# Nine output stores moved from SyncE's queue to GpSimd's in a fused convolution and spectral-mix kernel

## The chip, the cores and the metric

The kernel runs on one core of a Trainium2 chip. The metric is the device time of one launch in microseconds; lower is better. Before the change the median of 7 runs is 176.81 us (176.29 to 177.27).

## What is computed

The inputs are `x` (8 sequences of 3264 positions, 192 channels, float32), `weight` (8 heads, 7 taps) and three matrices of a spectral layer: `w_r` and `w_i` (64 modes, each 192 x 192) and `w_ch` (192 x 192). A causal convolution along the sequence comes first, with the softmax of each head's taps. On its result `x` the spectral layer does this:

```python
X = np.fft.rfft(x, axis=1)
Xr, Xi = (np.real(X[:, :n_modes]), np.imag(X[:, :n_modes]))
Yr = np.einsum('bmd,mde->bme', Xr, w_r) - np.einsum('bmd,mde->bme', Xi, w_i)
Yi = np.einsum('bmd,mde->bme', Xr, w_i) + np.einsum('bmd,mde->bme', Xi, w_r)
Y[:, :n_modes] = Yr + 1j * Yi
y = np.fft.irfft(Y, n=S, axis=1)
u = x + y
return (u + np.maximum(u @ w_ch, 0.0)).astype(np.float32)
```

The output is 8 x 3264 x 192 in float32, 20.05 MB. It is written by the stores that this document is about.

## The kernel before

The 8 sequences are handled as 4 pairs (q = 0 to 3, two sequences each). A sequence has 25 full tiles of 128 positions and one half tile of 64.

The kernel has three stages. First `x` is loaded (line 177), the convolution runs on TensorE (line 351), and the forward transform is collected (line 377) while the convolved tiles stay in SBUF as `xall`. Then the modes' matrices are loaded (line 474) and applied (line 491). Both kinds of load are issued by GpSimd, and the last of them is issued at 96.8 us of the profiled execution. The output stage begins at about 110 us.

The output stage is a loop over 54 items, written out by hand in program order (lines 763 to 786). An item is a bank pair `z` of PSUM. TensorE puts `u @ w_ch` there in two parts (`c_part`, line 576, and the first `m_part`, line 596), ScalarE applies the relu in place (line 661), TensorE adds `y` (the second `m_part`), and `finish(n)` (line 663) lets VectorE add the convolved `x` and write the float32 result to an SBUF buffer, which is then stored. There are four `z`, so TensorE works some items ahead. The items, with the index `n` that the texts use:

- n = 0 and 1: one tile of a pair of sequences, stored by SyncE (line 684), 192 KB each.
- n = 2, 3, 4: the first double tiles. Two neighbouring tiles of one pair; each is stored by two transfers of 192 KB, one for each sequence, issued by SyncE (line 699).
- n = 5 to 51, except 23 and 38: the same tile of two pairs of sequences, stored by one transfer of 384 KB that GpSimd issues (line 694). There are 45 of these. Item 23 has no output (it finishes a table of the inverse transform).
- n = 38, called "h": the half tiles of all 8 sequences. It is stored by four transfers of 96 KB, each from 64 partitions, issued by SyncE (line 675).
- n = 52 and 53: single tiles. Item 52 is stored by GpSimd, item 53 by SyncE (both line 684).

What sets the order around the change: each engine takes its instructions in program order. A store waits on its own engine's queue until VectorE has written the item's buffer (line 686, for "h" line 667). Stores of GpSimd have a further condition: the built program gives eight semaphores in turn to the transfers that GpSimd issues, so that a transfer also waits until the one eight places earlier in that queue has landed. SyncE's transfers have eight semaphores of their own. Buffers of the results (6 at first, 11 at the end, `free` and `LATER`, lines 647 to 656) are used in turn, so VectorE can write into one only when its previous store has landed.

Of the kernel before, what the change touches and what calls it, by code (L numbers as in the profile page):

```python
# [19 lines left out]
def kernel(  # L20
# [9 lines left out]
    nc = tc.nc  # L30
# [137 lines left out]
    def slot(q, t):  # L168
        return NT * q + t
# [55 lines left out]
    for g in range(4):  # L225
        dst, srcv = band[32 * g:32 * g + 32, :, 32 * g:32 * g + PW], pk3[32 * g:32 * g + 32, :, :]
# [225 lines left out]
    for k, u in enumerate(units):  # L452
# [7 lines left out]
        if k:  # L460
            q, t0, n = units[k - 1]
# [196 lines left out]
    def relu(n):  # L658
        duo, zt = items[n]
        w = D * len(duo) if duo[0] != "h" else 2 * D  # L660
        nc.scalar.activation(out=zt[:, :, 0:w], in_=zt[:, :, 0:w], func=ACT.Relu)  # L661

    def finish(n):
        duo, zt = items[n]
        o = buffers[n]
        if duo[0] == "h":
            nc.vector.tensor_tensor(out=o[:, :, :].rearrange("p k (a d) -> p k a d", a=2),
                                    in0=zt[:, :, 0:2 * D].rearrange("p k (a d) -> p k a d", a=2),
                                    in1=xall[:, NF:NF + NT * (NQ - 1) + 1:NT, 0, :].rearrange(
                                        "p (k a) d -> p k a d", k=2), op=ALU.add)  # L670
            for k in range(2):
                for h, r in enumerate(ROWS):
                    dst = bass.AP(tensor=out.tensor, offset=out.offset + ((4 * k + (h ^ k)) * S + P * NF) * D,
                                  ap=[[D, HALF], [2 * S * D, 2], [1, D]])
                    nc.sync.dma_start(out=dst, in_=o[r, k, :].rearrange("p (a d) -> p a d", a=2))
            return
        (q0, t0), (q1, t1) = duo[0], duo[-1]
        s = [slot(*u) for u in duo]
        ov = o[:, :, :].rearrange("p k (i d) -> p (k i) d", i=2)
        if len(duo) == 1:  # L680
            nc.vector.tensor_tensor(out=ov[:, 0:2, :], in0=zt[:, :, 0:D], in1=xall[:, s[0], :, :], op=ALU.add)
            dst = bass.AP(tensor=out.tensor, offset=out.offset + (2 * q0 * S + P * t0) * D,
                          ap=[[D, P], [S * D, 2], [1, D]])
            (nc.sync if n < 2 or n == N - 1 else nc.gpsimd).dma_start(out=dst, in_=ov[:, 0:2, :])
            return
        nc.vector.tensor_tensor(out=o[:, :, :].rearrange("p k (i d) -> p i k d", i=2),  # L686
                                in0=zt[:, :, 0:2 * D].rearrange("p i (k d) -> p i k d", k=2),
                                in1=xall[:, s[0]:s[1] + 1:s[1] - s[0], :, :].rearrange("p k i d -> p i k d"),
                                op=ALU.add)
        if t0 == t1:  # L690

            dst = bass.AP(tensor=out.tensor, offset=out.offset + (2 * q0 * S + P * t0) * D,
                          ap=[[D, P], [S * D, 4], [1, D]])
            nc.gpsimd.dma_start(out=dst, in_=ov)  # L694
        else:
            for i in range(2):
                dst = bass.AP(tensor=out.tensor, offset=out.offset + ((2 * q0 + i) * S + P * t0) * D,
                              ap=[[D, P], [P * D, 2], [1, D]])
                nc.sync.dma_start(out=dst, in_=ov[:, i:4:2, :])

    N = len(duos)
    items = [[duo, None] for duo in duos]
# [60 lines left out]
    for n in range(N + 1):  # L763
        if n < N and not is_zw(n):
            m_part(n, 0)
            relu(n)
        if n + 2 in AHEAD:
            nc.scalar.copy(out=four(items[n + 2][1][:, :, 0:2 * D]), in_=AHEAD[n + 2])
        elif given(n + 2):
            nc.scalar.copy(out=items[n + 2][1][:, :, 0:2 * D].rearrange("p k (a d) -> p k a d", a=2),  # L770
                           in_=halves.rearrange("p (k a) d -> p k a d", k=2))

        if n == 1:
            continue
        if n == 2:
            m_part(0, 1)
            finish(0)

        soon = given(n + 1) or given(n + 2) or given(n + 3) and not given(n - 1)
        if n > 1 and not soon and not given(n):  # L780
            set_up(n + 1)
        if 0 < n and not is_zw(n - 1):
            m_part(n - 1, 1)
            finish(n - 1)
        if n > 1 and soon:
            set_up(n + 2 if given(n + 1) else n + 1)
# [30 lines left out]
```

## Time and profile before

| | us |
|---|---|
| median of 7 runs | 176.81 |
| time of the profiled execution | 176.29 |
| its span, from the first to the last instruction | 174.5 |
| last loads of the modes' matrices issued | 96.8 |
| first and last store issued by SyncE | 111.3, 167.7 |
| first and last store issued by GpSimd | 117.0, 167.8 |
| last work of TensorE and of VectorE | 166.8, 167.7 |

The profile is one execution seen by the hardware profiler. A row of the chain of waits gives the start, the length and the instruction; a row of the table by stretches of time gives each engine's busy time, the granted clock of TensorE, the share of time that the 16 DMA engines were busy, and what they moved. The view of a stretch's DMA queues gives packets, megabytes and the share of the 16 engines' time that the packets took; `software_dynamic` is what GpSimd issues, `hardware_dynamic` what SyncE issues. "Landing" is the time from the start of the issue to the moment when all data is in its place.

### The profile page before, as it was taken

Reading aid. Unit: us, or ns where it says so; the run is one execution under the profiler, and the core shown is the slowest. Engines: PE = TensorE matmul, PEld = TensorE weight load, DVE = VectorE, ACT = ScalarE, POOL = GpSimd, SP = SyncE. Lnnn points to the kernel's source line nnn. Section 1 sums busy time; section 2 is a strip of 40 time slices with the busy share of each in tenths; the row PEclk is TensorE's granted clock in tenths of the full one; section 3 lists DMA queues with packets and bytes.
Section 4 is the critical chain, followed back from the end, with each engine's and each line's share of the span. In section 5 each row is a group of like instructions: output and inputs, shape, how many; then the busy total and the mean of one; then the engine's idle time right before and its main releaser. Section 6 shows DMA issues by size and latency. Waiting matters only on the chain.

```text
span 174.5 us, 6496 instructions
## 1 busy us (share of the span) xinstructions
PE 155.7 (89%) x2818; PEld 112.1 (64%) x2818; DVE 120.6 (69%) x193; ACT 107.2 (61%) x159; POOL 90.4 (52%) x141
## 2 busy tenths in 40 slices
PE   7997989999999997999897696999999999999910
PEld 3554655676666676788674564887786788677700
DVE  1889996847666866466575362788898698788840
ACT  8429878355547335566655242788787787787710
POOL 7999852945634733425334200016758576656650
PEclk9999999999999999999999789999999999999995
DMA  3999999999999999999999991287888989999993
GB/s 45 163 174 192 188 193 191 192 193 193 192 193 193 197 207 207 209 203 207 206 207 206 207 197 25 73 291 308 348 343 331 365 332 358 357 325 353 363 359 131
DMA packets 44077, 40.19 MB, mean 230 GB/s; under 512 B 28544, under 2 KB 40400, under 8 KB 44048
## 3 DMA queue, kind: packets, MB, share of 16 engines
q0 software_dynamic: 40880, 37.58, 108.3%
q1 hardware_dynamic: 3168, 2.19, 3.9%
q8 instruction: 22, 0.36, 0.8%
q14 instruction: 7, 0.06, 0.1%
HBM read 39.40 MB, written 20.05 MB: 341 GB/s over the span
## 4 chain that ended last, share of the span: by engine, by line
DMA 45%; POOL 28%; issue 13%; PE 7%; ACT 1%; DVE 1%; POOLq 1%; ACTq 0%
DMA xall<-in_x_dram 20%; DMA arena<-in_moe_w_i_dram 18%; POOL out_dram L694 16%; POOL xall L177 8%; DMA cc<-in_moe_w_i_dram 7%; PE z L596 4%; PE z L576 3%; PE low L491 1%; ACT z L661 1%; POOL cc L474 1%; POOL xall L258 1%; POOL arena L474 1%; DVE cc L686 1%; POOL early L293 0%; POOLq L812 0%
## 5 line engine op out<-in xcount | busy, mean ns | idle before, releaser
L661 ACT ACTIVATE z<-z 128x768 f32<-128x768 f32 (+1 forms) x53 | 39.8, 770 | 10.3 <-PE z L596 9.4
L596 PE MATMUL z<-mixa,early 64*128 64x384 bf16 (+1 forms) x220 | 33.8, 309 | 0.5 <-ACT z L661 0.4
L596 PE MATMUL z<-mixa,fupper 64*128 64x384 bf16 (+1 forms) x220 | 33.7, 308 | 0.0
L177 POOL DMA_DIRECT2D xall<-in_x_dram x32 | 27.8, 876 | 11.2 <-DMA xall<-in_x_dram 10.2
L369 ACT CAST xall<-z 128x768 bf16<-128x768 f32 (+1 forms) x24 | 20.5, 852 | 19.9 <-PE z L351 19.9
L371 DVE CAST xall<-z 128x768 bf16<-128x768 f32 (+1 forms) x24 | 24.5, 1023 | 10.6 <-PE z L351 10.3
L576 PE MATMUL z<-wc,cc 64*128 64x192 bf16 x504 | 28.4, 243 | 0.0
L351 PE MATMUL z<-xall,band 64*64 64x192 bf16 (+3 forms) x816 | 25.4, 249 | 2.3 <-ACT xall L369 1.4
L576 PEld LDWEIGHTS <-cc 64*128 64x128 bf16 x504 | 22.8, 94 | 5.6 <-issue 2.1
L686 DVE TENSOR_TENSOR arena<-z,xall 128x768 f32<-128x768 f32 x24 | 22.9, 957 | 3.3 <-PE z L596 1.5
L351 PEld LDWEIGHTS <-band 64*64 64x64 bf16 x816 | 16.8, 105 | 10.4 <-issue 5.6
L377 PE MATMUL low<-xall,early 128*128 128x384 bf16 x100 | 20.4, 329 | 0.2 <-ACT early L248 0.2
L686 DVE TENSOR_TENSOR cc<-z,xall 128x768 f32<-128x768 f32 x19 | 18.1, 956 | 3.4 <-PE z L596 2.1
L432 PEld LDWEIGHTS <-xall 128*128 128x128 bf16 x300 | 18.2, 103 | 2.8
L694 POOL DMA_DIRECT2D out_dram<-arena x22 | 16.6, 754 | 6.3 <-DVE arena L686 5.3
L407 DVE COPY cc<-r 128x1024 bf16<-128x1024 bf16 (+2 forms) x22 | 13.3, 633 | 9.5 <-PE r L432 3.7
L694 POOL DMA_DIRECT2D out_dram<-cc x18 | 13.6, 754 | 9.1 <-DVE cc L686 7.2
L596 PEld LDWEIGHTS <-early 64*128 64x128 bf16 x220 | 14.3, 94 | 6.1 <-issue 2.2
L474 POOL DMA_DIRECT2D arena<-in_moe_w_r_dram x12 | 7.4, 613 | 18.3 <-PE low L491 14.6
L694 POOL DMA_DIRECT2D out_dram<-band x5 | 3.8, 759 | 21.0 <-DVE band L686 20.9
L405 ACT COPY cc<-r 128x1024 bf16<-128x1024 bf16 (+1 forms) x11 | 10.1, 915 | 6.2 <-PE r L432 4.0
L596 PEld LDWEIGHTS <-fupper 64*128 64x128 bf16 x220 | 12.1, 94 | 1.3 <-issue 0.2
(129 smaller groups left out, 211.5 us busy)
## 6 DMA issues: line engine op xcount, KB each, us to landing
out_dram<-arena POOLq DMA_DIRECT2D x22, 384.0 KB, 4.8
out_dram<-cc POOLq DMA_DIRECT2D x18, 384.0 KB, 4.8
arena<-in_moe_w_r_dram POOLq DMA_DIRECT2D x12, 288.0 KB, 9.2
arena<-in_moe_w_i_dram POOLq DMA_DIRECT2D x12, 288.0 KB, 10.0
xall<-in_x_dram POOLq DMA_DIRECT2D x6, 480.0 KB, 11.7
xall<-in_x_dram POOLq DMA_DIRECT2D x6, 384.0 KB, 11.2
out_dram<-band POOLq DMA_DIRECT2D x5, 384.0 KB, 4.4
xall<-in_x_dram POOLq DMA_DIRECT2D x8, 192.0 KB, 6.5
```

The source lines that it names most:

```text
L177: nc.gpsimd.dma_start(out=xall[:, s0:s0 + nf, i, :], in_=src)
L351: mm = nc.tensor.matmul(ov[c], band[r, h, c.start + shift + 64 * (r is UP and c is LO): c.start + shift + 64 * (r is UP and c is LO) + 64] ...
L369: nc.scalar.copy(out=dst, in_=srcv)
L371: nc.vector.tensor_copy(out=dst, in_=srcv)
L377: nc.tensor.matmul(xp, ftab[:, t, :], xall[:, slot(q, t), :, :], start=(t == 0), stop=False, skip_group_check=True)
L407: nc.vector.tensor_copy(out=out, in_=in_)
L432: nc.tensor.transpose(tp[:, P * k:P * k + P], src, ident[:])
L576: nc.tensor.matmul(zt[:, i, D * k:D * k + D], cc[r, q, 3 * t + j, :], wc[r, j, :], start=(k == 0 and j == 0), stop=False, skip_group_check ...
L596: nc.tensor.matmul(zt[:, i, D * k:D * (k + w)], tabs[c][r, t, :], zw[r, c, q:q + w, QUARTERS[which], :], start=False, stop=end and k + w = ...
L661: nc.scalar.activation(out=zt[:, :, 0:w], in_=zt[:, :, 0:w], func=ACT.Relu)
L686: nc.vector.tensor_tensor(out=o[:, :, :].rearrange("p k (i d) -> p i k d", i=2), in0=zt[:, :, 0:2 * D].rearrange("p i (k d) -> p i k d", k=2),
L694: nc.gpsimd.dma_start(out=dst, in_=ov)
```

## The change

Nine stores change the engine that issues them. Of the six stores of the items 2, 3 and 4, five go to GpSimd; the first of item 2 stays with SyncE. The four stores of "h" are no longer issued when the item is finished: they are held in a list, and each following call of `finish` (items 39, 40, 41 and 42) lets GpSimd issue one of them just ahead of that item's own store. Nothing else changes: the instructions of TensorE, VectorE and ScalarE are the same in the same order.

```diff
+    held = []
+
     def finish(n):
         duo, zt = items[n]
         o = buffers[n]
@@ -672,8 +675,11 @@
                 for h, r in enumerate(ROWS):
                     dst = bass.AP(tensor=out.tensor, offset=out.offset + ((4 * k + (h ^ k)) * S + P * NF) * D,
                                   ap=[[D, HALF], [2 * S * D, 2], [1, D]])
-                    nc.sync.dma_start(out=dst, in_=o[r, k, :].rearrange("p (a d) -> p a d", a=2))
+                    held.append((dst, o[r, k, :].rearrange("p (a d) -> p a d", a=2)))
             return
+        if held:
+            dst, src = held.pop(0)
+            nc.gpsimd.dma_start(out=dst, in_=src)
         (q0, t0), (q1, t1) = duo[0], duo[-1]
         s = [slot(*u) for u in duo]
         ov = o[:, :, :].rearrange("p k (i d) -> p (k i) d", i=2)
@@ -696,7 +702,7 @@
             for i in range(2):
                 dst = bass.AP(tensor=out.tensor, offset=out.offset + ((2 * q0 + i) * S + P * t0) * D,
                               ap=[[D, P], [P * D, 2], [1, D]])
-                nc.sync.dma_start(out=dst, in_=ov[:, i:4:2, :])
+                (nc.sync if n == 2 and i == 0 else nc.gpsimd).dma_start(out=dst, in_=ov[:, i:4:2, :])
```

## The prediction, made before the changed kernel was run

> **What bounds the kernel now.** I read the page's 40 slices first, then a table of stretches, the chain of waits of the last 25 us, and the DMA queues of single stretches. From 110 us on TensorE is never idle until 166, so it sets the pace of the items; but the span ends only at 174.5. What carries the end is in this table (the columns are busy us with counts, then the granted clock, DMA share and GB/s):
>
> ```profile
> 140.00:152.00 12.00, 12.00 (x200) 8.84 (x196) 10.00 (x12) 9.71 (x13) 7.94 (x12) 1.00 0.93 351
> 154.00:158.00 4.00, 4.00 (x66) 3.01 (x63) 3.24 (x4) 3.44 (x6) 2.24 (x3) 1.00 0.97 325
> 160.00:167.00 7.00, 6.34 (x104) 4.62 (x99) 6.07 (x8) 5.00 (x8) 4.92 (x7) 1.00 0.97 361
> 167.00:172.00 5.00, 0.00 (x0) 0.00 (x0) 0.69 (x2) 0.00 (x0) 1.46 (x2) 0.79 0.91 337
> ```
>
> From 154 us the DMA engines are busy 0.97 of the time, with GpSimd (fifth number) far from full; after 167 nothing works but they, until the last landing near 173.0 (item 52: issued at 167.80, landed 5.1 us later). Then 1.5 us of closing waits. So the end is the drain of a backlog of stores, and TensorE's granted clock is 1.00 as long as it works, so no clock is in play. The second row is odd: as busy as the third, but 325 GB/s in place of 361. It holds the half-tile stores. The chain of waits shows GpSimd's issues there:
>
> ```profile
> 153.98 0.75 POOL out_dram L694
> ...
> 155.01 0.75 POOL out_dram L694
> ...
> 156.16 0.75 POOL out_dram L694
> 156.91 1.24 issue
> 158.14 0.02 POOLq L694
> 158.16 0.53 POOL out_dram L694
> ```
>
> These are items 39 to 42. Asked one by one, their landings took 3.9, 5.5, 5.3 and 4.3 us: they land at 157.9, 160.5, 161.5, 162.5. Items before and after land 1.0 us apart; between 39 and 40 lie 2.55 us. So the half tiles hold up the backlog by 1.55 us, and from there on it never empties: a landing takes 3.5 us where little is queued (item 5, at 117.0), 3.9 for item 39, but 4.3 to 5.5 for all later ones. Why they are so dear is in the queues of three stretches: 112 to 117.5 (SyncE's stores alone), 140 to 150 (GpSimd's alone), 154 to 158 (both):
>
> ```profile
> q1 hardware_dynamic: 2141, 1.55, 84.1%
> ...
> q0 software_dynamic: 970, 3.44, 89.9%
> ...
> q0 software_dynamic: 252, 0.90, 61.4%
> q1 hardware_dynamic: 567, 0.39, 34.5%
> ```
>
> Megabytes over share times length is the rate while engines serve that queue: SyncE's 1.55/(0.841 x 5.5) = 335 GB/s in packets of some 720 B, GpSimd's 3.44/(0.899 x 10) = 383 GB/s in packets of some 3,550 B. Mixed, both are worse: 366 for GpSimd's, 283 for SyncE's.
>
> **Part 1, five early stores (items 2, 3, 4).** SyncE loses five issues, GpSimd gains five of 192 KB; the row for that shape is line 684's issue on GpSimd, 0.71 us. Sum 3.6 us, where GpSimd has been idle since 97.5 us and would first issue at 117.0. VectorE's results are there at 113.0, 114.2 and 115.3, an issue follows 0.28 us later, so the five run at 113.3, 114.5, 115.2, 115.9 and 116.6, and item 5's store starts at 117.3 in place of 117.0. Item 6's (118.1) is on time again. Landings come later: 1.9 to 3.7 us now, 3.5 then (item 5's row). Nobody waits for that: the buffer of item 2 is written again at 119.8 and that of item 3 at 121.1, against landings before 117.6 and 119.5. In the built program's waits these five wait in addition only for weight loads that landed by 107. Cheaper packets save 0.98 MB/335 - 0.98/383 = 0.4 us of DMA time, but at a time when the DMA engines have gaps, and the backlog empties at 130 anyway (the store at 129.99 lands in 2.9 us). I count 0. If item 5's 0.3 us were carried through, the cost is +0.3; below zero there is nothing to gain, since TensorE sets the pace there.
>
> **Part 2, four half-tile stores: issue.** GpSimd gains four issues. The nearest row is line 258's, the same 64 x 2 x 192 shape as a load: 0.604 to 0.647 us; the other bound is 0.71. I take 0.61. Now every instruction past which they are put: item 38's result is there at 152.82. Half 1 runs 153.1 to 153.7; item 39 at 153.98, unmoved; half 2 to 155.34; item 40 at 155.34 (+0.34); half 3 at 156.1; item 41 at 156.7 (+0.56); half 4 at 157.5; item 42 at 158.08, where it starts at 158.16 now, since GpSimd stood idle before it for 1.24 us though VectorE's result was there at 157.2. Items 43 to 46 follow at 158.8, 159.6, 160.45, 161.58: the old times within 0.1. So the 2.4 us of issue fit into GpSimd's gaps, and nothing is late from item 42 on. At 0.71 each, item 42 starts at 158.2 to 158.3, still level.
>
> The waits on the transfer eight places earlier: the tightest is item 46's at 161.6 for item 40's landing, at the latest 160.5. SyncE's last store (item 53, 167.7) has nothing before it in either version. VectorE reuses item 38's buffer near item 49 (163.95); half 4 lands near 161.
>
> **Part 3, the same stores: transfer.** 4 x 96 KB = 0.393 MB at 283 GB/s is 1.39 us of all 16 engines now, at 383 it is 1.03: 0.36 saved. GpSimd's own 0.90 MB of that stretch go at 366 and would go at 383: 2.46 - 2.35 = 0.11. Together 0.47 us out of a backlog that ends the span. The landings say the same from the other side: 1.55 us now against 1.03, so 0.52. I take 0.47.
>
> Here the Trainium skill speaks against the change. "DMA: Bandwidth & Descriptors", section "Issuing engine by pattern", gives a simple store to SyncE's queue as the generally faster one, and its section "Issuing engines are not separate DMA queues" holds that whoever issues, the transfers run on the same 16 engines, so that only issue time is at stake. By it Part 3 is worth 0 and the sum is 0 or a little above. By the rows the engines are the same, but a byte of SyncE's stores occupies them 14% longer (335 against 383 GB/s), 35% longer in the contested stretch. I follow the rows, since the stretch and shape are this kernel's own; untested is that 64-partition stores keep 383 when GpSimd issues them. The bounds for that: 283 (saving only the 0.11) to 383.
>
> **Sum.** 0 (early) + 0 (issue) - 0.47 (transfer) = -0.47 us; span 174.5 to 174.0. The profiled execution took 176.29, 1.8 more than its span, and the median is 0.52 above it; so 175.82 for a like execution, 176.34 for the median.
>
> **Rivals.**
> - No change: the saving is returned. Item 42 is issued no earlier than now (158.08 against 158.16), and the DMA engines can only finish early what has been issued. If 4.3 us is what a landing costs at that load, not 3.9, item 42 lands at 162.4 as now and the tail is the same. Against it: landings of 3.9 and 4.1 (item 37) just before. Without the saving's reach the sum is 0 to -0.1: 176.8.
> - Slower: GpSimd falls behind between items 39 and 42. Twice now it stood still though VectorE's result was there: at 128.65 (issued at 129.99) and at 157.20 (issued at 158.16), about 1.0 and 0.7 us beyond the usual 0.28. I can't name the cause; nine more transfers in the queue may move the place. Today such a pause falls into slack. With four half tiles in the queue there is none: a pause of 1.0 us at item 39 makes item 42 start at 159.1, landing at 159.1 + 3.9 = 163.0 against 162.5. From there the tail keeps its 1.0 us per store, so +0.5 us, 177.3; with 4.3 for the landing +0.9. It decides from a start of item 42 after 158.6 (162.5 - 3.9).
> - The change fails to do what it says: excluded for the order (the built program has the nine transfers in GpSimd's queue as told); that the saving isn't there since the half tiles are slow by their 64 partitions gives -0.1, as the first rival.
>
> **Numbers.** Forecast (saving reaches the end, -0.3 to -0.7): 0.46. No change (within 0.3): 0.29. GpSimd behind (+0.4 to +1.0): 0.25. A measurement of this kernel can tell about 0.2%, or 0.35 us, from no change. Faster by more than that 0.44, within 0.31, slower 0.25. The range takes in the transfer bounds below (176.34 - 0.4) and most of the third case above: 175.9 to 177.5. The likeliest case alone: 176.1 to 176.5.
>
> **What would show it.** Right: in 154 to 158 no packets of SyncE's queue and a rate near 350 GB/s; landings of items 40 to 42 near 4 us; item 42 issued by 158.3; last landing near 172.5. Wrong in Part 3: the same 325 GB/s with GpSimd's packets alone. Wrong in Part 2: gaps or issues of GpSimd that put item 42 past 158.6, and less DMA share in 154 to 160. Wrong in Part 1: VectorE waiting for a landing before 125 us. What would upset all: an item's add waiting for its buffer in the tail, which now never happens.

## The result, and the profile after

The changed kernel has a median of 178.23 us (177.72 to 181.32, 14 runs), against 176.81 for the kernel before (35 runs). The ratio is 1.0095 with an interval of 1.0071 to 1.0118: the change costs about 0.9%, some 1.4 to 1.7 us. The forecast was 176.34 us; the sign was wrong, and the time lies above the range.

Single executions of every kernel here, before's too, scatter by up to some 5 us, and the ratios leave out those more than 1.5% above the fastest of their kernel, which the medians keep. The profiled execution took 181.23 us with a span of 179.5. In it TensorE was granted half its clock from 108.5 to 115.3 us (0.50; in the second profile below 1.00 in the same stretch), just ahead of the output stage, and everything after it is later (VectorE's add of "h" ends at 156.64 in place of 152.82), so that traces are compared below from that add on. These are the stretches that the prediction showed, moved by the same 3.82 us (busy us with counts of PE, PEld, DVE, ACT, POOL, then the granted clock, DMA share and GB/s):

```profile
143.82:155.82 12.00, 12.00 (x200) 8.85 (x196) 10.00 (x12) 9.71 (x13) 7.94 (x12) 1.00 0.91 347
157.82:161.82 4.00, 4.00 (x66) 3.01 (x63) 3.24 (x4) 3.44 (x6) 4.00 (x7) 1.00 0.76 272
163.82:170.82 7.00, 6.34 (x104) 4.61 (x99) 6.07 (x8) 5.00 (x8) 5.32 (x8) 1.00 0.99 363
170.82:175.82 5.00, 0.00 (x0) 0.00 (x0) 0.69 (x2) 0.00 (x0) 1.46 (x2) 0.76 1.00 372
```

The second row tells it (its counterpart, 154:158, is in the prediction). TensorE, VectorE and ScalarE are as busy as before, to the digit. GpSimd went from 2.24 us of work to 4.00 of 4.00. The DMA share fell from 0.97 to 0.76, and the rate from 325 to 272 GB/s. Later the DMA engines are full to the end (0.99 and 1.00). What wasn't moved in the second stretch is moved at the end, after everybody else has stopped. The chain of waits has this for GpSimd:

```profile
155.66 0.75 POOL out_dram L700
156.41 1.18 issue
157.59 0.02 POOLq L700
157.61 0.62 POOL out_dram L682
158.23 0.65 POOL out_dram L700
```

GpSimd stands still for 1.18 us ahead of the first half tile, and from there on issues back to back until item 46's store. Of the 1.24 us at item 42 before, 0.66 were beyond the usual wait for VectorE; this excess has moved here. The queues of 157.82 to 161.82 show a single kind of store:

```profile
q0 software_dynamic: 337, 1.06, 72.4%
```

1.06 MB/(0.724 x 4 us) = 366 GB/s while the engines serve that queue. The two queues together made (0.90 + 0.39)/((0.614 + 0.345) x 4) = 336 before in the same stretch; over the longer stretches used below the gain is gone.

The changed kernel was profiled once more, in an execution without that disturbance (178.30 us, span 176.4). For it and for before, this is the table by which all runs are compared: the 8 us after the add of "h" ends, then the time from VectorE's last add to the end of the span, then two single microseconds, from 1.0 us after the add of "h" on. Before:

```profile
152.82:160.82 8.00, 8.00 (x136) 6.34 (x132) 7.00 (x8) 6.74 (x10) 4.88 (x7) 1.00 0.92 333
167.69:174.50 6.81, 0.00 (x0) 0.00 (x0) 0.00 (x1) 0.00 (x0) 0.82 (x2) 0.66 0.57 212
153.82:154.82 1.00, 1.00 (x18) 0.67 (x16) 0.89 (x1) 1.00 (x3) 0.75 (x1) 1.00 0.92 334
154.82:155.82 1.00, 1.00 (x19) 0.77 (x20) 0.92 (x1) 0.77 (x2) 0.75 (x1) 1.00 0.92 307
```

The changed kernel:

```profile
153.37:161.37 8.00, 8.00 (x136) 6.35 (x132) 7.00 (x8) 6.74 (x10) 7.04 (x11) 1.00 0.81 294
168.24:176.40 8.16, 0.00 (x0) 0.00 (x0) 0.00 (x1) 0.00 (x0) 0.82 (x2) 0.68 0.56 209
154.37:155.37 1.00, 1.00 (x18) 0.67 (x16) 0.89 (x1) 1.00 (x3) 1.00 (x2) 1.00 0.67 269
155.37:156.37 1.00, 1.00 (x19) 0.77 (x20) 0.92 (x1) 0.77 (x2) 1.00 (x3) 1.00 0.59 164
```

From the add of "h" to VectorE's last add it is 14.87 us in both. So nothing is late on the computing engines. GB/s times length says what had still to be moved at the last add: 212 x 6.81 = 1.44 MB before, 209 x 8.16 = 1.71 MB after. The last landing comes 5.26 us after the last add before, and 6.35 after: +1.09 us. Behind the landing lie closing waits, 1.57 us before and 1.85 in both executions of the changed kernel: +0.28. Together 1.37 us, close to the 1.42 between the medians. The first profile of the changed kernel gives 6.11 us for the last landing, with the same 1.71 MB left and 289 GB/s in its 8 us. So the bytes left repeat well, while a difference of 0.2 us in a last landing says nothing.

### The profile page after: what moved, and what is told of

It is laid out like the page before. It is cut to its first block, busy times and chain, and to the rows that moved or that the text cites. A ratio compares the mean times of both kernels' runs of the same rounds, so it can differ in the third digit from the quotient of the medians.

```text
span 179.5 us, 6498 instructions
## 1 busy us (share of the span) xinstructions
PE 157.4 (88%) x2818; PEld 113.2 (63%) x2818; DVE 120.6 (67%) x193; ACT 107.4 (60%) x159; POOL 96.5 (54%) x150
## 4 chain that ended last, share of the span: by engine, by line
DMA 49%; POOL 29%; issue 12%; PE 5%; POOLq 1%; DVE 1%; DVEq 0%
DMA xall<-in_x_dram 25%; POOL out_dram L700 18%; DMA arena<-in_moe_w_i_dram 17%; DMA cc<-in_moe_w_i_dram 7%; POOL xall L177 5%; PE z L596 2%; POOL out_dram L705 1%; PE z L576 1%; POOL out_dram L682 1%; PE low L491 1%; POOL cc L474 1%; POOL arena L474 1%; PE low L606 1%; DVE cc L692 1%; POOLq L818 0%
## 5 line engine op out<-in xcount | busy, mean ns | idle before, releaser
L596 PE MATMUL z<-mixa,early 64*128 64x384 bf16 (+1 forms) x220 | 34.6, 318 | 0.4 <-ACT z L661 0.4
L596 PE MATMUL z<-mixa,fupper 64*128 64x384 bf16 (+1 forms) x220 | 34.4, 317 | 0.0
L576 PE MATMUL z<-wc,cc 64*128 64x192 bf16 x504 | 29.3, 248 | 0.0
L576 PEld LDWEIGHTS <-cc 64*128 64x128 bf16 x504 | 23.5, 96 | 5.8 <-issue 2.4
L700 POOL DMA_DIRECT2D out_dram<-arena x22 | 16.6, 755 | 6.1 <-DVE arena L692 3.7
L705 POOL DMA_DIRECT2D out_dram<-arena x3 | 2.2, 729 | 18.2 <-DVE arena L692 18.2
```

The lines of the kernel that those rows point to most:

```text
L576: nc.tensor.matmul(zt[:, i, D * k:D * k + D], cc[r, q, 3 * t + j, :], wc[r, j, :], start=(k == 0 and j == 0), stop=False, skip_group_check ...
L596: nc.tensor.matmul(zt[:, i, D * k:D * (k + w)], tabs[c][r, t, :], zw[r, c, q:q + w, QUARTERS[which], :], start=False, stop=end and k + w = ...
```

## The experiments

**Theory at the outset.** The loss sits in the half tiles' part: on GpSimd their issues take the place of those of the following items, and the DMA engines get too little to do in the microseconds after the add of "h". **Rivals**: the early stores make it, or their sum with the half tiles does (GpSimd's pause moves); the half tiles are released too late, one by one; the stores of 64 partitions are dear in transfer, whoever issues them.

| kernel | median, us | ratio, interval | last landing after VectorE's last add, us | MB left at that add | GB/s in the 8 us after the add of "h" |
|---|---|---|---|---|---|
| before | 176.81 | | 5.26 | 1.44 | 333 |
| the change again | 178.03 | 1.0076 (1.0041 to 1.0112) | 6.35 | 1.71 | 294 |
| early stores only | 176.76 | 1.0012 (0.9981 to 1.0043) | 5.38 | 1.44 | 322 |
| half tiles only | 177.44 | 1.0022 (0.9995 to 1.0049) | 5.76 | 1.57 | 304 |
| one half tile store of four | 176.97 | 1.0021 (0.9999 to 1.0043) | 4.92 | 1.40 | 297 |
| eight early stores | 178.32 | 1.0085 (1.005 to 1.012) | 6.12 | 1.55 | 312 |
| half tiles in a burst | 177.37 | 1.0045 (1.0022 to 1.0067) | 6.02 | 1.58 | 303 |
| half tiles in eight stores | 178.75 | 1.0138 (1.0094 to 1.0181) | 8.05 | 2.21 | 277 |
| two half tiles on each engine | 177.75 | 1.0022 (0.9993 to 1.005) | 5.29 | 1.44 | 327 |
| half tiles held, on SyncE | 177.03 | 0.9998 (0.9971 to 1.0025) | 5.37 | 1.48 | 326 |
| three early stores | 179.87 | 1.0128 (1.0068 to 1.0188) | 6.95 | 1.80 | 281 |

The third column compares with runs of before on the same chip, whose median was between 176.74 and 176.94. The last three columns come from one execution each. They are counted from the add of "h" or from the last add, so that what happens earlier doesn't touch them; how well they repeat is seen only for the change (6.11 and 6.35 us, 1.71 MB twice, 289 and 294 GB/s).

**The change again.** No edit.

> The changed kernel once more, for a profile whose TensorE clock is not held at half speed for 7 us before the output stage, as in the profile at hand (108 to 115 us). Both theories: 1.0 to 1.6 us above the kernel before. Theory A (the half tiles on GpSimd: the pause of its queue falls at the first half tile, then its issues run back to back until item 45): item 42's store starts about 0.4 us later against VectorE's last add than before, and the last landing comes 0.8 us later against that add. Theory B (the five early stores on GpSimd cost the time): a backlog is seen already between items 5 and 37, landings there longer than before's 4.6 to 4.9 us.

178.03 us; the tables above are from it. Item 42's store starts 9.18 us ahead of the last add, 0.36 later than before, about as expected; the last landing is 0.85 and 1.09 us later in the two profiles, where 0.8 was expected. The row of the half tiles' line 682 shows what its four issues cost (shortest, median and longest in ns):

```profile
L682 POOL DMA_DIRECT2D out_dram<-arena x4: 612/616/621, 154.3 to 158.5; - x4
```

The same view of line 690, whose longest landing is that of item 52 (5.1 before):

```profile
DMA to landing us min/median/max: 2.1/4.2/6.2
```

**Early stores only.**

```diff
-                nc.sync.dma_start(out=dst, in_=ov[:, i:4:2, :])
+                (nc.sync if n == 2 and i == 0 else nc.gpsimd).dma_start(out=dst, in_=ov[:, i:4:2, :])
```

> Only the five stores of items 2, 3 and 4 go to GpSimd; the half tiles stay with SyncE. Theory A: within 0.3 us of the kernel before, since the backlog empties before item 37. It may cost up to 0.8 if the pause of GpSimd's queue, moved to about item 39 by five more transfers, falls where it is not hidden. Theory B: the whole 1.2 to 1.5 us.

176.76 us: no change that can be measured. GpSimd's timeline (start, length, and in brackets the idle time before it and what ended it) at the beginning, and at item 39:

```profile
113.29 0.73 POOL L699 DMA_DIRECT2D out_dram<-arena  x1 [16.18 <-DVE arena L686]
114.46 1.46 POOL L699 DMA_DIRECT2D out_dram<-cc  x2 [0.43 <-DVE cc L686]
115.91 1.45 POOL L699 DMA_DIRECT2D out_dram<-arena  x2
117.36 0.77 POOL L694 DMA_DIRECT2D out_dram<-band  x1
...
154.61 0.75 POOL L694 DMA_DIRECT2D out_dram<-cc  x1 [2.06 <-DVE cc L686]
```

The five issues fill the time up to item 5's store at 117.36, and nothing comes of it at the end. But the pause has moved. Item 39 before the change:

```profile
153.98 0.75 POOL L694 DMA_DIRECT2D out_dram<-cc  x1 [1.39 <-DVE cc L686]
```

GpSimd is now idle for 0.67 us more ahead of item 39, and item 42 waits 0.59 us in place of 1.25. It does no harm here: 1.44 MB are left at the last add, as before. SyncE hands half tiles to the DMA engines in the meantime.

**Half tiles only.** The early stores go back to SyncE; the half tiles stay as in the change.

```diff
-                (nc.sync if n == 2 and i == 0 else nc.gpsimd).dma_start(out=dst, in_=ov[:, i:4:2, :])
+                nc.sync.dma_start(out=dst, in_=ov[:, i:4:2, :])
```

> Only the four half tiles go to GpSimd, one ahead of each of items 39 to 42; the early stores stay with SyncE. Theory A: the greater part of the loss, 0.8 to 1.5 us above the kernel before. Theory B: within 0.3 us of before, or 0.5 faster if the transfer saving of the prediction holds.

177.44 us, less above before than the 0.8 to 1.5 us expected. The ratio's interval takes in 1. The trace has 0.50 us more after the last add, and the lower rate and the bytes left point the same way; the burst below, with the same bytes left, is slower than before beyond its interval.

```profile
152.99:160.99 8.00, 8.00 (x136) 6.32 (x132) 7.00 (x8) 6.74 (x10) 7.32 (x11) 1.00 0.84 304
167.86:175.08 7.22, 0.00 (x0) 0.00 (x0) 0.00 (x0) 0.00 (x0) 0.82 (x2) 0.61 0.59 218
```

So the half tiles cost without the early stores, and the early stores cost nothing that can be measured without the half tiles, but the two together cost more than their sum (0.85 and 1.09 at the last landing against 0.50 + 0.12; 0.27 MB left over before's against 0.13 + 0).

**One half tile store of four.** Before, with three of the four half-tile stores left out, so that this part of the output isn't written.

```diff
-                    nc.sync.dma_start(out=dst, in_=o[r, k, :].rearrange("p (a d) -> p a d", a=2))
+                    if k == 0 and h == 0:
+                        nc.sync.dma_start(out=dst, in_=o[r, k, :].rearrange("p (a d) -> p a d", a=2))
```

> The kernel before with three of the four half-tile stores left out, so that this part of the output is not written; it shows what these stores cost the end when SyncE issues them. If the backlog from the half tiles reaches the end, three quarters of the 1.55 us that the landings showed: 1.0 to 1.2 us faster than before. If the backlog at the end is made later, between items 42 and 53, less than 0.4 us faster.

176.97 us: leaving out 0.29 MB of stores gives nothing that can be measured in the time, and 0.34 us at the last landing of the one profile. The prediction had taken the half tiles for 1.55 us of backlog that is carried to the end. It isn't carried: at the last add 1.40 MB are left, against 1.44.

```profile
168.22:174.70 6.48, 0.00 (x0) 0.00 (x0) 0.00 (x1) 0.00 (x0) 0.82 (x2) 0.67 0.57 216
```

Before the change the DMA engines make good by then what the half tiles add, so that a cheaper transfer of the half tiles could hardly have won 0.47 us.

**Half tiles in a burst.** As half tiles only, with all four issues ahead of item 39's store.

```diff
-        if held:
+        while held:
```

> Half tiles on GpSimd, all four ahead of item 39's store; the early stores on SyncE. Theory A': item 39's store starts 1.5 us later than before and GpSimd's issues bring 160 GB/s for 2.4 us, but from item 42 on the queue is where the interleaved one is: same loss as with one by one, 0.3 to 0.7 us above the kernel before. Rival (the interleaving itself costs): back at the kernel before.

177.37 us, 6.02 after the last add. All four half tiles are released at once, and it is no better than one by one (5.76). These are the four issues here, SyncE's four before, and the microsecond of the burst in which the DMA engines have least to do:

```profile
153.93 2.41 POOL L682 DMA_DIRECT2D out_dram<-arena  x4 [0.53 <-DVE arena L670]
...
152.85 2.67 SPq L675 DMA_DIRECT2D out_dram<-arena  x4
...
156.64:157.64 1.00, 1.00 (x22) 0.85 (x20) 0.62 (x2) 0.96 (x2) 1.00 (x2) 1.00 0.57 136
```

Counted from the add of "h" (153.64 and 152.82) GpSimd's issues end at 2.70 us, and so do SyncE's. The half tiles are no later, and still the kernel is slower: the rival "released too late" falls. With either order GpSimd spends four times 0.6 us on 96 KB each, and the hole in the DMA engines' work only changes its place.

**Half tiles in eight stores.** As half tiles only, each store cut in two of 48 KB, two ahead of each item.

```diff
-                    held.append((dst, o[r, k, :].rearrange("p (a d) -> p a d", a=2)))
+                    src = o[r, k, :].rearrange("p (a d) -> p a d", a=2)
+                    held.append([(dst[:, a:a + 1, :], src[:, a:a + 1, :]) for a in range(2)])
...
-            dst, src = held.pop(0)
-            nc.gpsimd.dma_start(out=dst, in_=src)
+            for dst, src in held.pop(0):
+                nc.gpsimd.dma_start(out=dst, in_=src)
```

> Half tiles on GpSimd cut into eight stores of 48 KB, two ahead of each of items 39 to 42: the bytes are the same, the issue time of GpSimd is doubled (2.4 us more). Theory A': less is moved in the 8 us after the add, by 300 to 500 KB more than with four; 1.5 to 2.2 us above the kernel before. Rival (the cost is in the transfers, not in their issue): within 0.4 us of the half tiles alone.

178.75 us, 8.05 after the last add: the same bytes in twice as many issues cost 2.79 us there in place of 0.50. Eight issues of about 0.53 us take 4.3 us of GpSimd's time in place of 2.5. Over the 8 us only 0.22 MB less are moved than with four (277 against 304 GB/s), where 0.3 to 0.5 were expected; but GpSimd is behind to the end, and at the last add 0.64 MB more are left. A new wait comes on top:

```profile
158.78 0.53 POOL L683 DMA_DIRECT2D out_dram<-arena  x1
159.78 0.54 POOL L683 DMA_DIRECT2D out_dram<-arena  x1 [0.46 <-DMA out_dram<-cc]
160.59 0.77 POOL L701 DMA_DIRECT2D out_dram<-cc  x1 [0.28 <-DVE arena L693]
```

The last half tile waits 0.46 us for a landing: the condition on the transfer eight places earlier, which with small stores in the queue reaches less far back in time.

**Two half tiles on each engine.** The two stores of `k` = 0 stay with SyncE, the two of `k` = 1 go to GpSimd ahead of the items 39 and 40; the early stores stay with SyncE. The list and its use are those of the change (not shown).

```diff
-                    nc.sync.dma_start(out=dst, in_=o[r, k, :].rearrange("p (a d) -> p a d", a=2))
+                    src = o[r, k, :].rearrange("p (a d) -> p a d", a=2)
+                    if k == 0:
+                        nc.sync.dma_start(out=dst, in_=src)
+                    else:
+                        held.append((dst, src))
```

> Two half tiles by SyncE as in the kernel before, two by GpSimd ahead of items 39 and 40; the early stores on SyncE. Theory A': GpSimd has slack for two (1.2 us of issue against gaps of 0.4 us per item); the loss is less than half of that of four: 0 to 0.3 us above the kernel before. Rival (64-partition stores on GpSimd's queue are slow in themselves): half, 0.3 us or more.

5.29 us after the last add, as before, and no difference in the ratio (the median of all 22 executions is 177.75 us, that of the 15 which the ratio takes 176.79). GpSimd's pause is seen at item 41 and costs nothing here:

```profile
157.28 1.50 POOL L704 DMA_DIRECT2D out_dram<-cc  x2 [0.71 <-issue]
```

Two of the four issues fit into GpSimd's gaps, so long as SyncE supplies the DMA engines beside it. It is no gain either.

**Half tiles held, on SyncE.** The order of the change, with SyncE as the issuer; the early stores go back to SyncE too (not shown).

```diff
-            nc.gpsimd.dma_start(out=dst, in_=src)
+            nc.sync.dma_start(out=dst, in_=src)
```

> The order alone: the half tiles' four stores stay with SyncE but are held and issued one by one when the items 39 to 42 are finished; the early stores stay with SyncE. Theory (the loss is GpSimd's issue time: its queue runs back to back and gives the DMA engines too few bytes in the 8 us after the half tiles' add): GpSimd is left alone, so 176.6 to 177.1, last landing 5.2 to 5.6 us after VectorE's last add, about 1.45 MB still to move at that add, and at least 2.5 MB in the 8 us after the half tiles' add. Rival (the loss is that the half tiles are released up to three items later, whoever issues them): 177.3 to 178.0, last landing 5.8 to 6.4, 1.6 MB or more still to move.

177.03 us, as before. It tells less than I had hoped: on SyncE's queue nothing stands between the four stores, so that the order in the program doesn't hold them back:

```profile
153.35 2.75 SPq L682 DMA_DIRECT2D out_dram<-arena  x4
```

They run one after the other from the add of "h" on, as before (152.85, 2.67 us). The run shows only that the order in the program by itself costs nothing; what speaks against the late release is the burst.

**Eight early stores.** The change, with the items 0 and 1 and the first store of item 2 on GpSimd too.

```diff
-            (nc.sync if n < 2 or n == N - 1 else nc.gpsimd).dma_start(out=dst, in_=ov[:, 0:2, :])
+            (nc.sync if n == N - 1 else nc.gpsimd).dma_start(out=dst, in_=ov[:, 0:2, :])
...
-                (nc.sync if n == 2 and i == 0 else nc.gpsimd).dma_start(out=dst, in_=ov[:, i:4:2, :])
+                nc.gpsimd.dma_start(out=dst, in_=ov[:, i:4:2, :])
```

> The changed kernel with three more early stores on GpSimd (items 0 and 1 and the first of item 2), which puts three more transfers ahead of the half tiles. Theory A' (the loss is idle time of the DMA engines in the 8 us after VectorE's add of the half tiles: first because GpSimd issues 96 KB in 0.6 us, second because the pause of GpSimd's queue of about 1.2 us, which comes 24 stores after the former one, falls on the first half tile): the pause moves to about item 36, ahead of the half tiles, so only the first part is left: 0.3 to 0.7 us above the kernel before, as with the half tiles alone. Rival (the early stores add to the loss by themselves, wherever the pause is): 1.2 us or more above, as the changed kernel or worse.

178.32 us: by the ratio 1.5 us above before, which is the rival's outcome (1.2 or more) and not the theory's (0.3 to 0.7). The executions lie in two groups, six from 177.36 to 178.32 and five from 179.43 to 180.53; the profiled one is of the second. The pause did move, to item 36:

```profile
153.48 0.75 POOL L700 DMA_DIRECT2D out_dram<-cc  x1 [1.06 <-DVE cc L692]
```

In half tiles only that item waits 0.39 us:

```profile
150.49 0.75 POOL L700 DMA_DIRECT2D out_dram<-cc  x1 [0.39 <-DVE cc L692]
```

So the pause is 0.67 again, this time ahead of the half tiles. By the bytes this kernel stands where half tiles only stands (1.55 MB left against 1.57), as the theory has it; but the time is that of the change, and the last landing comes 0.36 us later than in half tiles only. So the place of the pause isn't all.

**Three early stores.** The change, with only the second store of item 3 and both of item 4 on GpSimd.

```diff
-                (nc.sync if n == 2 and i == 0 else nc.gpsimd).dma_start(out=dst, in_=ov[:, i:4:2, :])
+                (nc.sync if n == 2 or n == 3 and i == 0 else nc.gpsimd).dma_start(out=dst, in_=ov[:, i:4:2, :])
```

> As the change, but only three of the early stores go to GpSimd (the second of item 3 and both of item 4); the half tiles on GpSimd one by one. The place of GpSimd's 0.68 us pause moves with the data that it has issued before: at the first half tile with five early stores, not seen with none. Theory (the pause among the half tiles makes the difference between 177.4 with none and 178.1 with five): the pause is seen between the second half tile and item 42, last landing 5.9 to 6.4 us after VectorE's last add, 177.8 to 178.4; if it isn't seen, 5.6 to 5.9 and 177.2 to 177.6. Rival (each early store on GpSimd costs by itself, 0.05 to 0.15 us): 177.6 to 177.9 wherever the pause is, and TensorE's last work relative to the first item's add is later than before.

179.87 us, in six runs only, two at 178.4 and four from 179.5 to 180.9; the median is above what theory (178.4 at most) and rival (177.9 at most) gave. 6.95 us after the last add, where five early stores have 6.11 and 6.35. The intervals of the two ratios overlap, so that it isn't shown that three cost more than five; but three don't cost less, and a price per early store is out. The pause is where the theory put it, behind the first half tile; the last line is item 39 in half tiles only:

```profile
155.98 0.62 POOL L682 DMA_DIRECT2D out_dram<-arena  x1 [0.53 <-DVE arena L670]
157.52 0.78 POOL L700 DMA_DIRECT2D out_dram<-cc  x1 [0.91 <-DVE cc L692]
158.29 0.62 POOL L682 DMA_DIRECT2D out_dram<-arena  x1
...
154.15 0.76 POOL L700 DMA_DIRECT2D out_dram<-cc  x1 [0.25 <-DVE cc L692]
```

GpSimd is idle ahead of item 39 for 0.91 us where half tiles only has 0.25: 0.66 more. What it does to the DMA engines:

```profile
155.69:163.69 8.00, 8.00 (x136) 6.34 (x132) 7.00 (x8) 6.74 (x10) 6.79 (x10) 1.00 0.78 281
170.56:179.08 8.52, 0.00 (x0) 0.00 (x0) 0.00 (x1) 0.00 (x0) 0.82 (x2) 0.60 0.57 211
157.70:158.70 1.00, 1.00 (x20) 0.77 (x21) 0.93 (x1) 0.76 (x2) 1.00 (x2) 1.00 0.17 54
```

For one microsecond the DMA engines are busy 0.17 of the time: in the 1.54 us between the issues at 155.98 and 157.52 only 96 KB had been handed to them.

## Why the prediction was wrong, step by step

**What bounds the kernel.** Half right. The span does end with a drain of stores (1.44 MB left at the last add). Wrong was the sentence "the half tiles hold up the backlog by 1.55 us, and from there on it never empties". I read it from landing times of 3.9 to 5.5 us. But a landing is the last of 16 engines: of item 42's data before the change, by the completions that the trace holds, one for each engine, half of the engines had finished 2.8 us after the issue began, and the last at 4.3. The landing told of the slowest engine, not of a store of work on all. The run with one half tile store of four shows what three of the four stores carried to the end: 0.34 us in its profile, and nothing that can be measured in the time.

**Part 1, five early stores: 0.** Right, and close: 113.3, 114.5, 115.2, 115.9, 116.6 and item 5 at 117.3 were predicted; the run with early stores only has 113.29, 114.46, pairs from there to 117.36, and an unchanged time. What was set aside is that these stores move GpSimd's pause.

**Part 2, issue: 0.** This is the step that failed, in its sentence "So the 2.4 us of issue fit into GpSimd's gaps, and nothing is late from item 42 on". Its numbers were nearly right: 0.61 us for an issue (measured 0.616), and in half tiles only the train of issues ran as written to within 0.3 us, item 42 starting 9.46 us ahead of the last add, against 9.53 before. It still cost 0.50 us at the last landing. The mistake was to ask only when GpSimd is level again. Before, SyncE issued the half tiles in 152.85 to 155.52, beside GpSimd's stores of the items 39 and 40; two queues fed the DMA engines. Afterwards GpSimd alone hands over 96 KB in 0.62 us, 160 GB/s, and such issues stand between its large ones. The DMA engines had no backlog to live on (with three early stores their share fell from 0.90 in one microsecond to 0.17 in the next), so that with half tiles only it fell at once, over the 8 us from 0.92 to 0.84. Of the 0.23 MB that were not moved then, 0.13 are still missing at the last add: (1.57 - 1.44) MB at 363 GB/s is 0.36 of the 0.50 us.

**The slower rival** had the right place and mechanism: the pause at item 42 "may move the place", and "with four half tiles in the queue there is none" of the slack that covered it. Its size is near too (+0.5 to +0.9 predicted; from half tiles only to the two profiles of the change +0.35 and +0.59 at the last landing). Its deciding point failed: it asked for item 42 after 158.6, that is less than 9.09 us ahead of the last add, and in the two profiles of the changed kernel that was 9.18 and 9.16 (8.92 only with three early stores). A late start of item 42 isn't needed; too little handed over ahead of it is enough. And the rival took the place of a gain, where in fact it came on top of the half tiles' own loss.

**Part 3, transfer: -0.47.** The second step that failed: the gain isn't there. Rates while the engines are busy, over the 8 us: before (2.26 + 0.39) MB/((0.739 + 0.178) x 8 us) = 361 GB/s, with these rows:

```profile
q0 software_dynamic: 643, 2.26, 73.9%
q1 hardware_dynamic: 576, 0.39, 17.8%
```

Half tiles only has 2.40/(0.835 x 8) = 359, the change 2.33/(0.792 x 8) = 368; the prediction counted on 383. So the half tiles are hardly cheaper with GpSimd's packets than with SyncE's 576. The 283 GB/s that I took for SyncE's came from a stretch of 4 us in which both queues' packets share the engines, and their times include each other's; it was no price of the stores. Even a true saving would have won little, as the run with one store of four shows.

The two sections of the Trainium skill's "DMA: Bandwidth & Descriptors" that I weighed and set aside were nearer: "Issuing engines are not separate DMA queues" has only issue time at stake, and so it was, 361 against 359 to 368 GB/s in transfer, though it calls that time usually small beside the transfer, and here it made the loss; and the simple store did belong on SyncE's queue ("Issuing engine by pattern").

**The sum**, measured on the changed kernel at the last landing: 0.12 from early stores alone, 0.50 from half tiles alone, 0.47 from the two together (0.23 by the first profile); and 0.28 in the closing waits, in place of -0.47.

**What stays open.** GpSimd's pause adds 0.66 to 0.71 us wherever it is seen (item 42 before; item 39, the first half tile, item 36, item 39 again, and item 41 with two half tiles on each engine), and its place follows the amount issued by GpSimd: from one pause to the next lie 24 stores of 384 KB, or 23 and one or two half tiles. In the two kernels with four half tiles and no early store on GpSimd (and in the one with eight) it wasn't seen a second time. What makes it isn't known. It also never fell among four half tiles without early stores on GpSimd, so that the times alone can't tell the pause from the early stores; what speaks for the pause is the hole of 0.17 just where it lies. The bytes left at the last add explain 0.27 MB at 363 GB/s, 0.74 us, of the change's 1.09, 0.99 of 1.69 us with three early stores, and only 0.30 of 0.86 with eight. Much of the rest is with the slowest engines. The trace has the time at which each of the 16 was done with item 52's data; counted from the last add, their mean is 4.35 us before, 4.27 with early stores only, 4.64 with half tiles only, 4.91 in both profiles of the change, 5.25 with three early stores and 4.53 with eight. As a whole the engines are 0.56 us later in the change, and only 0.18 with eight early stores; why the last of them falls behind by more was not tried. And the 0.28 us of closing waits appeared in both executions of the changed kernel, with 1.46 to 1.69 in all others; its cause wasn't tried.

## What to carry to other kernels

Before a transfer is moved to another engine's queue, ask who feeds the DMA engines in just those microseconds: bytes per issue over time per issue is a supply rate, and a small store on a queue that also issues the large ones takes their place, while on an idle queue it runs beside them. That the moved engine is level again some items later says nothing; look at the DMA share in stretches of one microsecond around the change, and count what is left to move when the computing ends. A long landing time is no proof of a backlog, since it is that of the slowest engine; leaving the stores out tells what they are worth.

## What the runs showed of the hardware that I had not expected

- A GpSimd issue has a price that hardly falls with its size: 0.75 us for 384 KB, 0.71 to 0.73 for 192 KB, 0.62 for 96 KB, 0.53 for 48 KB (the last two from 64 partitions, the others from 128). As supply that is 524, 274, 160 and 93 GB/s, against some 360 GB/s that the DMA engines move here. (SyncE's four issues of 96 KB took 2.67 us, no less, but on a queue with nothing else in it.)
- GpSimd's queue paused twice in the output stage, the second time by some 0.67 us and about 24 stores of 384 KB after the first, in nine of the twelve profiles; in three it paused only once. With all four half tiles on GpSimd in four stores, the last landing came 5.76 and 6.02 us after the last add where the second pause wasn't seen, and 6.11 to 6.95 where it was.
- Small packets were no burden: with SyncE's 576 packets of some 680 bytes among GpSimd's of some 3,500, the DMA engines moved 361 GB/s while busy, and 359 to 368 without them.
